# Moving the causal mask of two half batches from TensorE to GpSimd in a fused attention and gated-convolution kernel

## The chip, the cores and the metric

The kernel runs on one core of a Trainium2 chip. A core has a matrix engine (TensorE; PE in the profile, with its weight loads as PEld), a vector engine (VectorE, DVE), an activation engine (ScalarE, ACT), a general engine (GpSimd, POOL), and a queue engine that here only issues transfers (SyncE, SP). Each takes its own instructions in the order written and waits on semaphores for the others. Working tiles lie in SBUF; matrix products land in PSUM, from where ACT or DVE fetch them. POOL reads and writes SBUF only here. The metric is the device time of one execution, in microseconds (us).

## What is computed

Eight batches, eight heads, 576 positions, head width 64. The attention has a decay that is worked out from a forget gate `f`, and a causal mask; its output goes through a feed-forward layer with a three-tap convolution along the sequence and a sigmoid gate.

```python
cum = np.cumsum(np.log(np.clip(f, 0.0001, 1.0)), axis=-1)
scores = scale * q @ k.T + cum[:, None] - cum[None, :]
attn = softmax(np.where(causal, -1e9, scores)) @ v
h = np.maximum(attn @ w_in, 0.0)
conv = w0 * h[s - 1] + w1 * h[s] + w2 * h[s + 1]
out = (h * sigmoid(conv)) @ w_out
```

(Shortened: per head for the attention, per channel for the convolution.)

## The kernel before

Work is cut into 16 half batches of four heads each (`hb`), and each half batch into two pairs of heads, numbered `i = 2*hb` and `2*hb + 1`. The scores are made transposed (keys on partitions, queries along the free axis) in blocks of 128 by 128, and only the blocks on or below the diagonal are made. For each pair there are three batches of scores: `sd` holds the diagonal blocks (two heads, 1024 columns), `so...0` and `so...1` hold the off-diagonal blocks of one head each. For each half batch `st` holds the last 64 positions against themselves for all four heads (256 columns). ACT takes the exponential of each out of PSUM: `ed`, `eo`, `et`. Then `pv` multiplies the result with the values `v`, in two parts (`pv6.0`, `pv6.1`); `n` normalises on DVE; `t` and `tx` transpose the outcome for the feed-forward part. A value tile is first cast to 16 bits by `va`, on the engine that the order names (`va6.0@POOL`).

Only diagonal blocks need the mask. Two ways to apply it are in the code, and `MASK_PE` lists the half batches that use the first:

- on TensorE ahead of the scores: `masked` (line 367) writes a product of an identity and a mask matrix of very negative numbers into PSUM, and the scores are added on top. For a half batch that is four products of 512 columns and one of 256. The exponential then writes the 16-bit tile that `pv` reads.
- on GpSimd behind the exponential: `ed` and `et` write 32-bit tiles instead (`pd_t`, two of them; `p3_t`, two of them), and `md` (line 403) and `mt` (line 382) copy these to the 16-bit tile with zeros in place of what is masked. `pv` then waits for `md` and `mt` instead of `ed` and `et`.

Before the change half batches 0 to 7 use the first way and 8 to 15 the second.

The feed-forward part of each batch is `f` (first product), `r` (relu on ACT), `c` and `d` (the two steps of the convolution on DVE), `a` (tanh on ACT), `g` (gate on DVE), `o` (second product), `e` (copy out of PSUM) and `s` (store).

The order of all this work is a list written out by hand, `ORDER`. Each engine gets its instructions in the order of that list; there is no other scheduler. Buffers are handed out as the list is gone through: `Plan.play` keeps a list of free buffers per kind, a task takes the first free one, and a task that gives one back appends it to the end. PSUM has four buffers (`ps`), `pd` has two, `p3` two. Waits between engines follow from which instruction reads or writes which part of which buffer, transfers included.

Two small buffers live inside larger tiles. `cwrow`, the convolution weights as loaded, lies in `pd_t[0]` and is read at the start. `signs`, two rows of plus and minus ones, lies in `pd_t[1]`:

```python
signs = pd_t[1].rearrange("p s c -> p (s c)").bitcast(BF16)
plus, minus = (signs[0:BH, x * S:(x + 1) * S] for x in range(2))
```

The task `zc` (lines 330 and 331) sends them to a table in DRAM, with transfers issued by GpSimd; from that table, and from a block of zeros sent by the same task, the half batches from 8 on fill rows of their score operands (`fi8` and following, lines 241 and 243, issued by SP):

```python
for j, a, c in ((1, 0, plus), (2, 0, plus), (0, 1, minus), (3, 0, zero[:, 0:S]), (3, 1, zero[:, 0:S])):
    nc.gpsimd.dma_start(image[j, a], c)
nc.gpsimd.dma_start(blank, zero[0:60])
```

Of the kernel before, what the change touches and what calls it, by code (L numbers as in the profile page):

```python
# [17 lines left out]
dca cw ld0 ld0.0.0 tp0.0.0 dcl ld0.1.0 ld0.0.1 tp0.0.1 tp0.1.0 v0.0 ld1 ld0.1.1 ld1.0.1 ld1.0.0 dcs dck q2.1 ki@SP
cl0.0.0@ACT cl0.0.1@ACT v0.4 cl0.1.0@ACT tp0.1.1 q2.0 cwt sd0 ed0 cl0.1.1@DVE tp1.0.0 tp1.0.1 cl1.0.0@ACT cl1.0.1@DVE
tp1.1.0 tp1.1.1 cl1.1.1@ACT sd1 so1.0 eo1.0 cl1.1.0@DVE so0.0 so1.1 rw1 sd2 eo0.0 v0.1 ed1 cl2.1 cl2.0 eo1.1 v0.2 ed2  # L20
v0.3 va1.0@DVE va1.1@DVE rw2 wi1 sd3 so2.0 ed3 so3.1 eo3.1 va0.0@POOL va0.1@POOL so0.1 eo0.1 so3.0 wi0 eo3.0 st0 eo2.0
et0 so2.1 eo2.1 pv0.0 st1 n0.0 et1 q3.0 pv0.1 n0.1 pv1.0 pv1.1 n1.0 n1.1 wic0@ACT wi3 sd4 wic1@POOL ed4 t0 tx0@DVE t1
tx1@DVE sd5 cl3.0 q3.1 cl3.1 so5.1 eo5.1 f0.0 r0.0 f0.1 c0.0 wic3@POOL d0.0 st2 r0.1 ed5 et2 c0.1 d0.1 so4.0 eo4.0 wi2
f0.2 r0.2 v1.0 v1.3 v1.1 wic2@POOL c0.2 d0.2 h0 a0.0 g0.0 v1.4 f0.3 v1.2 f0.4 a0.1 r0.4 f0.5 f0.6 r0.5 va2.0@ACT rw3
sd6 q5.0 so4.1 g0.1 va3.0@DVE q5.1 r0.3 r0.6 c0.5 c0.3 so5.0 c0.4 sd7 d0.4 wo1 ed6 eo5.0 st3 et3 eo4.1 d0.5 cl5.0 a0.2
so7.1 ed7 eo7.1 pv2.0 so7.0 va2.1@DVE pv2.1 cl5.1 n2.0 q4.1 d0.3 va3.1@POOL eo7.0 wo2 rw5 so6.1 eo6.1 woc2@POOL g0.2
so6.0 cl4.1 eo6.0 q4.0 f0.7 r0.7 wo0 woc1@ACT pv3.0 a0.3 a0.5 n2.1 t2 q6.0 n3.0 tx2@ACT c0.7 g0.5 pv3.1 n3.1 a0.4 g0.3
sd11 ed11 so11.1 eo11.1 sd10 so10.1 eo10.1 ed10 cl4.0 rw4 wo3 woc0@ACT t3 tx3@DVE f1.0 r1.0 d0.7 a0.7 c0.6 d0.6 a0.6
f1.1 r1.1 f1.2 g0.4 so11.0 c1.0 v2.0 d1.0 sd8 f1.3 g0.6 r1.2 eo11.0 ed8 cl6.0 g0.7 q6.1 v2.2 r1.3 sd9 ed9 c1.3 d1.3
so8.0 v2.1 f1.4 r1.4 c1.4 d1.4 h1 a1.0 woc3@POOL o0.0 g1.0 eo8.0 cl6.1 st5 et5 a1.4 c1.1 g1.4 d1.1 so10.0 eo10.0 f1.5  # L30
a1.3 g1.3 so9.1 eo9.1 v2.3 va5.0@DVE r1.5 c1.5 d1.5 o0.1 e0.0@ACT f1.6 r1.6 f1.7 r1.7 st4 so9.0 eo9.0 a1.1 va4.0@DVE
pv5.0 q7.0 cl7.0 v2.4 so8.1 va5.1@POOL pv5.1 et4 eo8.1 rw6 q7.1 va4.1@ACT n5.0 sd13 v3.0 v3.4 pv4.0 n5.1 pv4.1 ed13 zc
n4.0 n4.1 a1.5 v3.1 so13.1 sd12 eo13.1 cl7.1 ed12 c1.2 t5 so12.0 eo12.0 t4 tx4@ACT tx5@ACT o0.2 q9.0 c1.7 d1.7 so12.1
eo12.1 a1.7 rw7 o0.3 c1.6 e0.1@ACT f2.0 f2.1 d1.2 d1.6 so13.0 a1.2 g1.5 g1.7 r2.0 f2.2 f2.3 r2.1 q8.1 eo13.0 g1.2 c2.0
st7 a1.6 o0.4 r2.3 g1.1 v3.2 v3.3 q9.1 et7 sd15 d2.0 r2.2 h2 c2.1 a2.0 e0.2@DVE so15.0 so15.1 ed15 g1.6 eo15.0 sd14
ed14 so14.0 eo14.0 f2.4 r2.4 f2.5 va6.0@POOL pv6.0 c2.3 d2.3 q8.0 c2.2 g2.0 so14.1 r2.5 o1.0 eo15.1 va7.0@DVE
va7.1@ACT d2.2 c2.4 st6 eo14.1 pv7.0 a2.2 et6 va6.1@DVE n6.0 pv6.1 d2.1 a2.1 d2.4 n7.0 v4.0 fi9 s0.2 v4.1 c2.5 s0.0
v4.4 fi8 q10.0 s0.1 a2.4 v4.3 n6.1 v4.2 g2.2 o1.1 e1.0@ACT pv7.1 sd19 f2.6 f2.7 q11.0 q10.1 g2.4 ed19 n7.1 r2.6 c2.6
d2.6 r2.7 sd18 ed18 t6 q11.1 t7 o1.2 tx6@DVE tx7@ACT a2.6 a2.3 d2.5 a2.5 g2.1 st9 f3.0 et9 g2.3 f3.1 so19.1 c2.7 d2.7
r3.0 r3.1 a2.7 md19 sd17 ed17 o1.3 f3.2 g2.6 g2.5 c3.0 so19.0 eo19.1 e1.1@DVE r3.2 eo19.0 d3.0 c3.2 o1.4 e1.2@DVE s1.2  # L40
c3.1 d3.1 md18 st8 s1.0 g2.7 fi10 so18.0 fi11 et8 f3.3 va9.0@DVE va9.1@ACT md17 s1.1 v5.0 eo18.0 so17.0 so18.1 h3 d3.2
a3.0 r3.3 eo17.0 a3.1 f3.4 f3.5 f3.6 g3.1 v5.3 v5.1 r3.5 g3.0 o2.0 a3.2 g3.2 c3.3 r3.4 r3.6 sd16 f3.7 eo18.1 mt8 ed16
so16.1 eo16.1 r3.7 d3.3 a3.3 c3.4 d3.4 v5.2 c3.7 d3.7 c3.6 so16.0 eo16.0 o2.1 e2.0@ACT a3.4 pv9.0 a3.7 va8.0@ACT
so17.1 q12.0 n9.0 md16 va8.1@ACT q12.1 eo17.1 o2.2 o2.3 e2.1@ACT st10 et10 c3.5 d3.5 d3.6 mt9 g3.4 pv9.1 n9.1 mt10
pv8.0 pv8.1 a3.5 n8.0 a3.6 n8.1 o2.4 g3.7 q13.0 g3.5 v5.4 e2.2@ACT fi12 s2.2 sd22 ed22 sd20 ed20 md22 t8 tx8@DVE t9
tx9@DVE g3.6 g3.3 q13.1 so20.0 md20 sd23 so22.1 eo20.0 ed23 sd21 md23 va11.0@DVE ed21 f4.0 r4.0 c4.0 d4.0 f4.1 f4.2
r4.1 eo22.1 f4.3 c4.1 r4.2 r4.3 so23.1 eo23.1 h4 so21.1 d4.1 a4.0 g4.0 so23.0 f4.4 r4.4 eo21.1 c4.2 a4.1 s2.1 o3.0
eo23.0 f4.5 v6.0 r4.5 f4.6 d4.2 a4.2 so22.0 md21 g4.1 fi13 eo22.0 c4.4 va11.1@DVE st11 et11 s2.0 mt11 o3.1 c4.5 d4.5
v6.3 so21.0 r4.6 o3.2 v6.1 v6.2 a4.5 so20.1 q14.1 q14.0 eo21.0 e3.0@ACT d4.4 f4.7 eo20.1 c4.6 g4.5 r4.7 sd24 a4.4
pv11.0 ed24 sd25 o3.3 c4.3 d4.3 g4.2 c4.7 d4.7 so25.1 md24 n11.0 pv11.1 ed25 e3.1@ACT va10.0@POOL eo25.1 a4.7 pv10.0  # L50
st12 d4.6 va10.1@POOL pv10.1 et12 sd27 n11.1 n10.0 n10.1 ed27 g4.7 o3.4 t10 e3.2@ACT a4.6 a4.3 t11 sd26 tx10@DVE
tx11@DVE md27 v6.4 ed26 so25.0 so27.1 g4.6 eo27.1 f5.0 f5.1 so26.0 q15.0 r5.0 c5.0 g4.3 d5.0 eo25.0 r5.1 c5.1 f5.2
so24.0 eo26.0 f5.3 f5.4 r5.2 eo24.0 r5.3 g4.4 o4.0 so26.1 so27.0 h5 a5.0 fi14 d5.1 a5.1 r5.4 eo27.0 c5.3 g5.0 d5.3
eo26.1 c5.4 c5.2 s3.2 q15.1 d5.2 so24.1 d5.4 eo24.1 a5.2 g5.1 va12.0@DVE o4.1 f5.5 st13 et13 va12.1@ACT g5.2 f5.6 md25
mt12 md26 r5.5 c5.5 d5.5 f5.7 r5.6 sd28 e4.0@ACT r5.7 c5.7 ed28 pv12.0 n12.0 so28.1 o4.2 pv12.1 a5.5 g5.5 va13.0@ACT
pv13.0 eo28.1 d5.7 a5.3 mt13 sd29 s3.0 md28 o4.3 va13.1@POOL n12.1 ed29 md29 c5.6 n13.0 fi15 pv13.1 a5.4 g5.4 e4.1@ACT
s4.1 n13.1 sd31 ed31 md31 sd30 t12 ed30 d5.6 md30 t13 o4.4 a5.6 tx12@DVE tx13@DVE so31.0 st14 a5.7 g5.6 g5.3 f6.0 et14
mt14 v7.0 eo31.0 r6.0 c6.0 f6.1 r6.1 c6.1 d6.0 f6.2 r6.2 e4.2@ACT so31.1 eo31.1 f6.3 so29.0 so29.1 g5.7 f6.4 r6.3 c6.2
d6.1 d6.2 eo29.0 r6.4 v7.2 c6.4 eo29.1 d6.4 o5.0 so28.0 o5.1 s4.0 h6 a6.1 eo28.0 g6.1 a6.2 st15 f6.5 v7.3 a6.0
e5.0@ACT et15 mt15 s3.1 c6.3 v7.1 va14.0@DVE pv14.0 v7.4 so30.0 s4.2 g6.0 g6.2 r6.5 va15.0@POOL va15.1@ACT eo30.0  # L60
n14.0 so30.1 c6.5 eo30.1 f6.6 r6.6 f6.7 va14.1@POOL pv14.1 d6.5 a6.4 d6.3 n14.1 a6.3 pv15.0 pv15.1 t14 r6.7 c6.6 a6.5
o5.2 n15.0 n15.1 t15 tx14@ACT tx15@ACT c6.7 d6.7 a6.7 d6.6 o5.3 g6.3 g6.7 e5.1@ACT f7.0 f7.1 r7.0 f7.2 o5.4 g6.4 f7.3
g6.5 a6.6 r7.1 c7.0 d7.0 r7.2 e5.2@ACT r7.3 c7.1 d7.1 h7 a7.0 g6.6 c7.2 d7.2 f7.4 f7.5 f7.6 f7.7 g7.0 a7.1 g7.1 r7.6
r7.4 s5.2 o6.0 o6.1 o7.0.0 c7.6 c7.3 r7.5 d7.3 d7.6 a7.2 c7.4 d7.4 a7.3 e6.0@ACT s5.0 g7.3 c7.5 a7.4 g7.2 o6.2 o6.3
o6.4 r7.7 c7.7 d7.5 g7.4 s6.0 o7.2.0 o7.3.0 o7.0.1 o7.0.2 a7.6 o7.2.1 o7.1.0 o7.2.2 e6.1@ACT d7.7 o7.2.3 s5.1 o7.1.1
o7.3.1 o7.1.2 o7.1.3 e6.2@ACT o7.0.3 o7.1.4 o7.2.4 a7.5 g7.6 g7.5 o7.2.5 a7.7 s6.2 s6.1 g7.7 o7.1.5 o7.2.6 o7.2.7
e7.2@ACT s7.2 o7.0.4 o7.0.5 o7.0.6 o7.0.7 o7.1.6 o7.3.2 o7.1.7 e7.0@ACT s7.0 e7.1@DVE o7.3.3 o7.3.4 o7.3.5 o7.3.6
# [39 lines left out]
def kernel(  # L107
# [290 lines left out]
    def diag_exp(i):  # L398
        o = pair(i)[:, :, 0:512] if i // 2 in MASK_PE else pd_t[slot[f"ed{i}", "pd"]]
        nc.scalar.activation(o, ps_of(f"sd{i}").rearrange("p (s c) -> p s c", s=2), AF.Exp, scale=SCALE)  # L400
# [316 lines left out]
```

## Time and profile before

| | us |
|---|---|
| median of three runs | 250.18 (249.65 to 250.89) |
| the profiled execution, its own time | 250.38 |
| its span (first to last instruction) | 248.4 |
| PE busy | 232.6 |
| DVE busy | 215.3 |
| ACT busy | 213.0 |
| POOL busy | 46.2 |

The page of the profile gives busy time by engine, the span in 40 slices, the chain of work that ended last, and the costliest groups of instructions. The timeline lists single instructions or runs of equal ones with start, duration and, in brackets, idle time before them and what ended it. The stretches view gives busy time of each engine between two moments. A matmul's duration reaches past the start of the next, since matmuls are pipelined; the time that one takes up on PE is read from start to start.

### The profile page before, as it was taken

What the parts mean: (1) busy time and instruction counts of PE and PEld (TensorE: products, weight loads), DVE (VectorE), ACT (ScalarE), POOL (GpSimd) and SP (SyncE); (2) the same over time, 40 slices, a digit from 0 to 9 for tenths busy, and PEclk for the clock granted to TensorE, in tenths of its full rate; (3) what the DMA queues carried; (4) which work ended last, traced back from release to release, by engine and by line L of the source; (5) the groups of instructions that cost most, each with busy time, mean ns of one, the idle gap of its engine ahead of it and who ended that gap; (6) DMA issues with size and microseconds to landing.
All of it is one profiled execution on the core that took longest, in us unless ns stands there. A gap on an engine that the chain in (4) does not pass through costs nothing.

```text
span 248.4 us, 6681 instructions
## 1 busy us (share of the span) xinstructions
PE 232.6 (94%) x2768; PEld 150.9 (61%) x2768; DVE 215.3 (87%) x328; ACT 213.0 (86%) x288; POOL 46.2 (19%) x76
## 2 busy tenths in 40 slices
...
GB/s 198 302 193 193 239 211 231 186 271 203 247 212 180 235 198 250 268 219 218 218 261 253 216 174 268 224 235 160 220 229 5 163 305 2 3 3 106 129 145 191
DMA packets 114694, 48.22 MB, mean 194 GB/s; under 512 B 104034, under 2 KB 105250, under 8 KB 114664
## 3 DMA queue, kind: packets, MB, share of 16 engines
...
q0 software_dynamic: 208, 0.51, 0.6%
...
q14 instruction: 9, 0.07, 0.1%
...
## 4 chain that ended last, share of the span: by engine, by line
PE 65%; SPq 9%; DVE 9%; DMA 8%; ACT 3%; issue 3%; ACTq 0%; DVEq 0%
PE ps L504 21%; PE ps L473 19%; PE ps L359 11%; SPq L227 6%; PE ps L436 6%; DMA qk<-in_k_dram 3%; PE ps L508 3%; DVE u L488 3%; DMA qk<-in_q_dram 3%; DVE u L490 2%; DMA u<-in_f_dram 2%; PE ps L458 2%; PE ps L441 2%; DVE hg L497 2%; DVE qk L233 1%
## 5 line engine op out<-in xcount | busy, mean ns | idle before, releaser
L417 ACT ACTIVATE pp<-ps 128x1024 f16<-128x1024 f32 x64 | 65.5, 1044 | 4.9 <-PE ps L359 2.7
L473 PE MATMUL ps<-xt,w_in_f 128*128 128x512 f16 (+1 forms) x512 | 68.2, 286 | 1.0 <-ACT ht L483 0.3
L359 PE MATMUL ps<-qk 128*128 128x128 bf16 (+2 forms) x576 | 63.2, 240 | 1.7 <-DVE xm L450 0.6
L504 PE MATMUL ps<-w_out_f,hg 128*128 128x512 f16 x256 | 59.4, 379 | 0.0
L488 DVE SCALAR_TENSOR_TENSOR u<-ht,cwt 128x576 f32<-128x576 f16 x64 | 52.8, 832 | 2.5 <-ACT ht L483 2.4
L490 DVE SCALAR_TENSOR_TENSOR u<-ht,cwt,u 128x576 f32<-128x576 f16 x64 | 53.7, 852 | 1.4
L473 PEld LDWEIGHTS <-w_in_f 128*128 128x128 f16 x512 | 34.0, 98 | 30.4 <-issue 1.8
L493 ACT ACTIVATE hg<-u,cw 128x576 f16<-128x576 f32 x64 | 48.8, 784 | 2.9 <-DVE u L490 2.9
L497 DVE SCALAR_TENSOR_TENSOR hg<-hg,ht 128x576 f16<-128x576 f16 x64 | 50.3, 806 | 1.1 <-ACT hg L493 0.9
L359 PEld LDWEIGHTS <-qk 128*128 128x128 bf16 x576 | 39.2, 98 | 19.2 <-issue 3.4
L483 ACT ACTIVATE ht<-ps 128x576 f16<-128x576 f32 x64 | 41.2, 668 | 2.9 <-PE ps L473 2.8
L504 PEld LDWEIGHTS <-hg 128*128 128x128 f16 x256 | 24.0, 98 | 25.6 <-issue 0.2
L403 POOL TENSOR_SCALAR_AFFINE_SELECT pp<-pd 128x1024 f16<-128x1024 f32 x16 | 18.5, 1168 | 48.7 <-ACT pd L400 42.9
L450 DVE TENSOR_TENSOR xm<-ps,rc 128x896 f16<-128x896 f32 (+1 forms) x32 | 24.3, 758 | 1.1
L436 PE MATMUL ps<-va,pp 128*128 128x65 f16 x640 | 24.6, 193 | 0.6 <-ACT pp L417 0.4
L436 PEld LDWEIGHTS <-pp 128*128 128x128 f16 x640 | 22.4, 97 | 3.0 <-ACT pp L417 0.7
L400 ACT ACTIVATE pp<-ps 128x1024 f16<-128x1024 f32 x16 | 16.5, 1039 | 4.0 <-PE ps L359 3.0
L514 ACT COPY ob<-ps 128x1024 f32<-128x1024 f32 (+1 forms) x18 | 15.1, 839 | 4.0 <-PE ps L504 3.2
L400 ACT ACTIVATE pd<-ps 128x1024 f32<-128x1024 f32 x16 | 15.9, 1023 | 1.9 <-PE ps L359 1.9
L367 PE MATMUL ps<-mask,ident 128*128 128x512 bf16 (+1 forms) x40 | 14.5, 362 | 0.4 <-ACT xt L464 0.2
L233 DVE TENSOR_SCALAR qk<-qk,lim 128x2304 uint16<-128x2304 uint16 x12 | 10.5, 874 | 3.1 <-DMA qk<-in_q_dram 1.9
L382 POOL TENSOR_SCALAR_AFFINE_SELECT pt<-p 128x256 f16<-128x256 f32 x8 | 4.8, 594 | 38.6 <-ACT p L379 37.0
...
## 6 DMA issues: line engine op xcount, KB each, us to landing
vf<-in_v_dram SPq DMA_DIRECT2D x32, 256.0 KB, 4.9
...
out_dram<-ob SPq DMA_DIRECT2D x4, 256.0 KB, 2.1
...
```

The source lines that it names most:

```text
L359: nc.tensor.matmul(o, tk[:, h * S + k0:h * S + k0 + 128], tq[:, h * S + q0:h * S + q0 + n], start=first, stop=last and not by_matmul(hb, h))
L400: nc.scalar.activation(o, ps_of(f"sd{i}").rearrange("p (s c) -> p s c", s=2), AF.Exp, scale=SCALE)
L417: nc.scalar.activation(pair(i)[:, s, 512:1536], ps_of(f"so{i}.{s}"), AF.Exp, scale=SCALE)
L436: nc.tensor.matmul(ps[:, c:c + D + 1], block(hb, h, m, n), va[:, h, m, 0:D + 1], start=(m == 0), stop=(m == n))
L450: nc.vector.tensor_tensor(xm[:, CUT * D * u:CUT * D * u + nj * k * D].rearrange("p (j x d) -> p j x d", x=k, d=D), got[:, :, :, 0:D], r.un ...
L473: nc.tensor.matmul(ps[:, t0:t1], w_in_f16[:, cc, 128 * ff:128 * (ff + 1)], xt[:, cc, x:x + t1 - t0], start=(cc == 0), stop=(cc == NCC - 1))
L483: nc.scalar.activation(ht_of(b, ff)[:, 1:1 + S], ps_of(f"f{b}.{ff}")[:, 0:S], AF.Relu, scale=0.5)
L488: nc.vector.scalar_tensor_tensor(u, ht[:, 0:S], cwt[:, ff, 0:1], ht[:, 1:1 + S], op0=ALU.mult, op1=ALU.add)
L490: nc.vector.scalar_tensor_tensor(u, ht[:, 2:2 + S], cwt[:, ff, 1:2], u, op0=ALU.mult, op1=ALU.add)
L493: nc.scalar.activation(hg_of(b, ff), u_t[slot[f"c{b}.{ff}", "u"]], AF.Tanh, scale=cw[:, ff, 1:2])
L497: nc.vector.scalar_tensor_tensor(hv, hv, 1.0, ht_of(b, ff)[:, 1:1 + S], op0=ALU.add, op1=ALU.mult)
L504: nc.tensor.matmul(ps[:, 512 * (c % 2):512 * (c % 2 + 1)], hg_of(b, ff)[:, 128 * c:128 * (c + 1)], w_out_f16[:, ff, :], **kw)
```

## The change

Half batches 6 and 7 (pairs 12 to 15) go over from the first way of masking to the second. Ten mask products leave PE; four `md` and two `mt` are added on POOL; the four `ed` and two `et` write 32-bit tiles. Each new task stands in the order right behind the exponential that feeds it; every other task keeps its place relative to the rest. (The list is also written as one line instead of many; only the inserted names differ.)

```diff
-    MASK_PE = (0, 1, 2, 3, 4, 5, 6, 7)
+    MASK_PE = (0,1,2,3,4,5)

 ORDER, where names are inserted:
-va5.1@POOL pv5.1 ... sd13 ... pv4.0 n5.1 pv4.1 ed13 zc n4.0 n4.1 a1.5 v3.1 so13.1
+va5.1@POOL pv5.1 ... sd13 ... pv4.0 n5.1 pv4.1 ed13 md13 zc n4.0 n4.1 a1.5 v3.1 so13.1
-sd12 eo13.1 cl7.1 ed12 c1.2 t5 so12.0 eo12.0 t4 tx4@ACT tx5@ACT o0.2 q9.0
+sd12 eo13.1 cl7.1 ed12 md12 c1.2 t5 so12.0 eo12.0 t4 tx4@ACT tx5@ACT o0.2 q9.0
-st7 a1.6 o0.4 r2.3 g1.1 v3.2 v3.3 q9.1 et7 sd15 d2.0 r2.2 h2 c2.1 a2.0 e0.2@DVE so15.0 so15.1 ed15 g1.6
+st7 a1.6 o0.4 r2.3 g1.1 v3.2 v3.3 q9.1 et7 mt7 sd15 d2.0 r2.2 h2 c2.1 a2.0 e0.2@DVE so15.0 so15.1 ed15 md15 g1.6
-eo15.0 sd14 ed14 so14.0 eo14.0 f2.4 r2.4 f2.5 va6.0@POOL pv6.0
+eo15.0 sd14 ed14 md14 so14.0 eo14.0 f2.4 r2.4 f2.5 va6.0@POOL pv6.0
-st6 eo14.1 pv7.0 a2.2 et6 va6.1@DVE n6.0 pv6.1
+st6 eo14.1 pv7.0 a2.2 et6 mt6 va6.1@DVE n6.0 pv6.1
```

More of the change, by code (lines that the diff above doesn't have):

```diff
@@ L17 @@
 ORDER = """
[L18 to L67, printed above, removed]
```

2 lines of the change are left out of this document (1 added, 1 removed).

## The prediction

> **What bounds the kernel now.** I read the page first, then the stretches of four microseconds around half batches 6 and 7, then the timeline of each engine there.
>
> ```profile
> span 248.4 us, 6681 instructions
> PE 232.6 (94%) x2768; PEld 150.9 (61%) x2768; DVE 215.3 (87%) x328; ACT 213.0 (86%) x288; POOL 46.2 (19%) x76
> PE 65%; SPq 9%; DVE 9%; DMA 8%; ACT 3%; issue 3%; ACTq 0%; DVEq 0%
> ```
>
> The third line is the chain that ended last: TensorE carries most of it. What it loses behind the start it hardly gets back, since it is busy to the end. But the share is an average; in the stretch that the change touches a second engine is just as full:
>
> ```profile
> 84.00:88.00 4.00, 4.00 (x46) 2.84 (x43) 3.93 (x7) 3.43 (x5) 0.00 (x0) 1.00 1.14 208
> 88.00:92.00 4.00, 4.00 (x26) 2.01 (x25) 4.00 (x6) 4.00 (x6) 0.00 (x0) 1.00 0.94 189
> 92.00:96.00 4.00, 4.00 (x46) 2.54 (x45) 3.31 (x6) 4.00 (x7) 0.32 (x1) 1.00 1.13 225
> 96.00:100.00 4.00, 4.00 (x45) 2.68 (x40) 3.69 (x6) 3.94 (x6) 1.21 (x1) 1.00 1.16 250
> 100.00:104.00 4.00, 4.00 (x56) 2.55 (x53) 3.96 (x8) 4.00 (x7) 0.00 (x0) 1.00 1.00 237
> 104.00:108.00 4.00, 4.00 (x76) 2.78 (x74) 3.77 (x6) 2.64 (x5) 0.00 (x0) 1.00 1.16 316
> ```
>
> The columns after the stretch's length are PE, PEld, DVE, ACT and POOL busy, then PE's granted clock and the transfers' share. From 88 to 104 ACT works without a gap, as PE does: a delay of ACT delays everything, and time given to PE alone is worth nothing until ACT has room, from about 106.6 on. POOL is nearly idle.
>
> **The products taken away.** Eight mask products of 512 columns and two of 256 go.
>
> ```profile
> 81.29 0.38 PE L367 MATMUL ps<-mask,ident 128*128 128x512 bf16 x1
> 81.51 0.38 PE L359 MATMUL ps<-qk 128*128 128x128 bf16 x4
> 104.50 0.27 PE L367 MATMUL ps<-mask,ident 128*128 128x256 bf16 x1
> 104.61 0.28 PE L359 MATMUL ps<-qk 128*128 128x64 bf16 x4
> ```
>
> From start to start a large one takes 0.22 us, a small one 0.11: 8 x 0.22 + 2 x 0.11 = 1.98 us. Only the small one of `st6`, at 104.50, lies close to where ACT has room. The rest lies before or inside the stretch in which ACT is full, so I credit 0.1 us; the ends are 0 and 1.98.
>
> **The first new wait: the buffer with the signs.** This is the largest term. The diagonal exponentials now take `pd` buffers. `ed13` takes the first, `pd_t[0]`. `md13` stands ahead of `ed12` in the order and puts `pd_t[0]` back at the end of the list, so `ed12` takes `pd_t[1]`: the tile in which `signs` lies and from which `zc` sends three transfers. `ed12` overwrites it, so it must wait until these have landed. Before, nobody took a `pd` buffer until half batch 9, at 109.68. And `zc` itself comes later, since it is now queued behind `md13` on POOL, which waits for `ed13`. POOL and ACT before:
>
> ```profile
> 78.00 0.67 POOL L266 CAST va<-vf 64x256 f16<-64x256 f32 x1 [9.67 <-DMA vf<-in_v_dram]
> 78.62 2.22 POOL L330 DMA_DIRECT2D image<-pd  x3
> 95.68 1.53 POOL L264 CAST va<-vf 128x1024 f16<-128x1024 f32 x1 [12.99 <-PE ps L508]
> 110.78 1.10 POOL L403 TENSOR_SCALAR_AFFINE_SELECT pp<-pd 128x1024 f16<-128x1024 f32 x1 [13.57 <-ACT pd L400]
> ```
>
> ```profile
> 82.37 1.02 ACT L400 ACTIVATE pp<-ps 128x1024 f16<-128x1024 f32 x1
> 85.55 1.02 ACT L400 ACTIVATE pp<-ps 128x1024 f16<-128x1024 f32 x1
> 87.37 2.15 ACT L464 COPY xt<-ps 128x1152 f16<-128x1152 f16 x2
> 99.22 1.03 ACT L400 ACTIVATE pp<-ps 128x1024 f16<-128x1024 f32 x1
> 100.13 1.04 ACT L417 ACTIVATE pp<-ps 128x1024 f16<-128x1024 f32 x1
> 108.49 1.01 ACT L514 COPY ob<-ps 128x1024 f32<-128x1024 f32 x1 [1.85 <-PE ps L504]
> 109.68 1.02 ACT L400 ACTIVATE pd<-ps 128x1024 f32<-128x1024 f32 x1 [0.18 <-PE ps L359]
> ```
>
> ```profile
> L403 POOL TENSOR_SCALAR_AFFINE_SELECT pp<-pd x16: 1092/1097/1584, 110.8 to 196.5; 128x1024 f16<-128x1024 f32 x16
> L330 POOL DMA_DIRECT2D image<-pd x3: 526/715/998, 78.6 to 79.8; - x3
> DMA to landing us min/median/max: 3.0/3.9/4.9
> ```
>
> The rows of ACT at 82.37 and 85.55 are `ed13` and `ed12`; 99.22 is `ed14`, 100.13 `eo14.0`. `ed13` ends at 83.39. A select follows its exponential by 0.08 (109.68 + 1.02, then 110.78), so `md13` runs from 83.47 to 84.57. Then `zc`: its third transfer starts 1.2 us after its first (78.6 to 79.8), so near 85.7. The last line is the landing time of the five transfers of that line to the table, 3.0 to 4.9 us; I take the median, 3.9, as the third one's own 4.9 was the longest and other traffic differs from one moment to the next. It lands at 89.6, and `ed12` starts near 89.7 instead of 85.55: 4.1 us. The ends are 3.2 (landing 3.0) and 5.1 (landing 4.9), and 5.6 with the longest select.
>
> Behind `ed12` on ACT everything waits: `eo12.0`, the two copies at 87.37, the tanh and relu. TensorE waits too:
>
> ```profile
> 86.69 0.22 PE L459 MATMUL ps<-ident,xm 128*128 128x128 f16 x1
> 86.75 1.89 PE L504 MATMUL ps<-w_out_f,hg 128*128 128x512 f16 x8
> 99.39 2.12 PE L473 MATMUL ps<-xt,w_in_f 128*128 128x512 f16 x16
> 101.35 1.16 PE L436 MATMUL ps<-va,pp 128*128 128x65 f16 x32
> ```
>
> `o0.2`, at 86.75, takes the PSUM buffer that `ed12` empties; before, it started 0.18 after `ed12`'s end at 86.57. Now it starts near 90.9, 4.1 late. ACT has no gap up to 104 in which to catch up.
>
> The price of a GpSimd transfer can also be had elsewhere. The Trainium skill, DMA: Bandwidth & Descriptors, section on the anatomy of one DMA on the gpsimd path, fits about 2.0 us plus the bytes at 436 GB/s; for one of 72 KB that makes an estimated 2.2 us. By that the first wait would be 2.4 and not 4.1 us, and the time about 254.1. The trace's own transfers, 3.0 us at the least, speak against it.
>
> **The second new wait: the cast behind the selects.** In POOL's order `va6.0` (95.68) now stands behind `md15` and `md14`. `pv6.0`, at 101.35 on PE, needs it. In times of before, to which the first delay is added: `ed14` ends at 100.24 + 0.01, `md14` runs from 100.33 to 101.43, and `va6.0` follows. Casts of that form on POOL:
>
> ```profile
> L264 POOL CAST va<-vf x4: 1032/1284/1532, 25.0 to 209.8; 128x1024 f16<-128x1024 f32 x4
> L382 POOL TENSOR_SCALAR_AFFINE_SELECT pt<-p x8: 414/500/923, 122.6 to 209.4; 128x256 f16<-128x256 f32 x8
> ```
>
> With 1.28 it ends at 102.71, and `pv6.0` starts near 102.75: 1.4 late. The ends are 1.1 (cast of 1.03) and 1.7 (1.53). The relu products ahead of `pv6.0`, at 99.39, wait for `eo15.0` on ACT, so the missing mask products don't bring PE there sooner. Behind `pv6.0` stand `so14.1`, `o1.0`, `st6` and so on, and the 1.85 us for which ACT waited at 108.49 was a wait for PE: from here PE sets the pace, and the delay stays.
>
> **The smaller parts.** `mt6` now stands between `et6` and the last products of `pv6.1`, which follow a little later: 0.2 us, ends 0 and 0.5 (the select takes 0.41 to 0.92). `md12`, `md15`, `mt7` have microseconds until `pv6.0` and `pv7.0`; nothing. The exponentials cost the same (1.02 in either form above). The blocks of zeros that `zc` sends land 6 us later; the first reader is at 98.39 on SP:
>
> ```profile
> 82.14 0.55 POOL L331 DMA_DIRECT2D blank<-zero  x1
> 98.39 0.95 SPq L241 DMA_DIRECT2D qk<-blank  x1
> ```
>
> Issued near 88.0 and landed in the 4.9 us that the longest row above took, they are there by 93; without that cover it would cost at most what it is late. A select also slows a product on DVE that runs beside it:
>
> ```profile
> 107.28 0.81 DVE L488 SCALAR_TENSOR_TENSOR u<-ht,cwt 128x576 f32<-128x576 f16 x1
> 111.40 1.09 DVE L488 SCALAR_TENSOR_TENSOR u<-ht,cwt 128x576 f32<-128x576 f16 x1 [0.87 <-ACT ht L483]
> ```
>
> The second lies beside the select of 110.78: 0.28 more. `md15` and `md14` would cost DVE 0.6, and between 92 and 100 it is idle for 1.0 (3.31 and 3.69 of 4.00): covered; 0.6 if not.
>
> **The sum.** 4.1 + 1.4 + 0.2 - 0.1 = 5.6 us. The profiled execution took 250.38 (the span and 1.98 around it), so 256.0; the median is 0.20 lower: 255.8. Its own range: 3.2 + 1.1 - 1.5 (most of the products' gain after all) = 2.8, so 253.0, up to 5.6 + 1.7 + 0.5 = 7.8, so 258.0.
>
> **The rivals.** First, *TensorE comes back slow*. While `ed12` waits, PE has nothing to do: its last work ahead of `o0.2`, moved up by what the products leave free, ends near 86.4, and the next starts near 90.9, a gap of 4.5 us. The only such gap in the trace is at the start, before 6.41:
>
> ```profile
> 7.32 3.06 PE L213 MATMUL ps<-ident_b,hg 128*128 128x128 bf16 x27
> 13.75 2.44 PE L213 MATMUL ps<-ident_b,hg 128*128 128x128 bf16 x36
> ```
>
> The same transposes took (3.06 - 0.22) / 26 = 0.109 us each first and (2.44 - 0.22) / 35 = 0.063 later, though the granted clock is shown as 1.00 in both. Some 36 of these at 0.046 more are 1.7 us. If a gap of 4.5 us does the same, the sum is 7.3 and the time 257.5. Against it: the first gap was longer and nothing had run before. The Trainium skill, TensorE: Matmul & The Clock Gate, Part 1, has the rule: half clock after an idle window of about 3.4 us, until about 3.4 us of work; the window is free-running, so a gap of 4.5 need not hold a whole one. The slow transposes agree, the granted clock doesn't.
>
> Second, *the second wait is absorbed*: if PE comes to `pv6.0` late for another reason, such as a buffer of PSUM that ACT empties later than before, the cast is done by then and only the first wait counts: 255.8 - 1.4 = 254.4. For it: all of PE's products from `o0.2` on depend on an ACT that is full. Against it: `pv6.0` followed without a gap before.
>
> Third, *`ed12` doesn't wait*: the buffers come out the other way, or the transfers have read the signs early. Then only the second wait is left: 250.2 + 1.4 + 0.2 - 0.1 = 251.7. The hand-out of buffers speaks against it.
>
> Fourth, on the other side, *PE's own work decides*: the chain is PE's, each product taken from its queue comes off, 250.2 - 2.0 = 248.2. It needs PE alone to be the bound between 82 and 108, and it decides only if `ed12` waits less than the 2.0 us saved; with a transfer issued near 85.7, after `ed12`'s old start, and 3.0 at the least, it doesn't.
>
> **How the numbers follow.** My forecast 0.62, slow TensorE 0.18, second wait absorbed 0.07, no wait at `ed12` 0.07, faster 0.06. The three runs of before lie 0.5% apart, so 0.5% is about what can be told from no change. Faster 0.06; within 0.5% (251.4 and less) 0.05, from the low edge of the third; slower 0.89. The range 253.0 to 259.0 leaves out the last two (251.7 and 248.2), and the far ends of the others: less than 2 in 10.
>
> **What would show it.** Right: ACT idle for some 4 us ahead of the `ed12` row, ended by a transfer or POOL; PE idle as long ahead of `o0.2`; the `image<-pd` row some 6 us later on POOL; the cast `va6.0` behind two selects, and PE idle for about 1.4 ahead of `pv6.0`. Slow TensorE: `o0.2`'s eight products in some 3.5 us instead of 1.73. Wrong: no idle row on ACT between 83 and 91, or gaps on PE that are made good before 230.

## The result, and the profile after

The change makes the kernel slower: 258.65 us (median of four runs, 256.0 to 259.32) against 250.15, a ratio of 1.0318 with a 95% interval of 1.0282 to 1.0355. The profiled execution took 258.59 us with a span of 256.8, 8.4 more than before. A ratio, here and below, leaves out executions more than 1.5% longer than the fastest of their kernel, which the medians include (with 24 added products on TensorE two of six were left). Below, lines are those of the kernel after, 50 lower than before (L350 is the diagonal exponential into `pd`, L353 the select, L280 the transfers of `zc`, L454 the second product of the feed-forward part, L214 the cast of the values, L438, L440 and L447 the two convolution steps and the gate on VectorE).

Four stretches, the first three of which are shown for before; columns: the stretch, its length, busy PE, PEld, DVE, ACT, POOL, granted clock, transfers' share and rate.

```profile
84.00:88.00 4.00, 2.14 (x32) 1.88 (x31) 3.93 (x7) 1.02 (x1) 3.55 (x7) 1.00 1.11 193
88.00:92.00 4.00, 1.13 (x3) 0.40 (x3) 3.03 (x5) 2.20 (x3) 1.10 (x1) 0.67 1.14 281
92.00:96.00 4.00, 4.00 (x13) 1.57 (x12) 0.00 (x0) 2.44 (x3) 0.00 (x0) 0.50 1.16 189
...
108.00:112.00 4.00, 2.06 (x41) 1.58 (x39) 4.00 (x5) 2.49 (x5) 1.92 (x2) 1.00 0.96 255
```

PE and ACT, full or nearly so before, are idle for more than half of the time from 84 to 92. The granted clock of PE, 1.00 in all these stretches before, falls to 0.67 and 0.50. A second hole on PE follows from 108 to 112. The timelines show what each is. ACT first:

```profile
81.88 1.04 ACT L350 ACTIVATE pd<-ps 128x1024 f32<-128x1024 f32 x1
...
89.80 1.02 ACT L350 ACTIVATE pd<-ps 128x1024 f32<-128x1024 f32 x1 [4.54 <-DMA image<-pd]
```

`ed12`, the row at 89.80, waited 4.54 us, for transfers out of `pd`. It is the only row of ACT that the trace puts down to a transfer of the signs. POOL and the landing times of its transfers:

```profile
83.00 1.10 POOL L353 TENSOR_SCALAR_AFFINE_SELECT pp<-pd 128x1024 f16<-128x1024 f32 x1 [3.94 <-ACT pd L350]
84.05 1.93 POOL L280 DMA_DIRECT2D image<-pd  x3
...
90.90 1.10 POOL L353 TENSOR_SCALAR_AFFINE_SELECT pp<-pd 128x1024 f16<-128x1024 f32 x1 [3.35 <-ACT pd L350]
...
106.85 1.57 POOL L353 TENSOR_SCALAR_AFFINE_SELECT pp<-pd 128x1024 f16<-128x1024 f32 x1 [0.73 <-ACT pd L350]
108.37 1.55 POOL L214 CAST va<-vf 128x1024 f16<-128x1024 f32 x1
```

```profile
L280 POOL DMA_DIRECT2D image<-pd x3: 526/706/715, 84.0 to 85.3; - x3
...
DMA to landing us min/median/max: 3.9/4.4/5.2
```

`md13` (83.00) stands ahead of the three transfers (84.05), the third of which starts at 85.3; `ed12` starts 4.5 us later. The selects `md15` and `md14` and then the cast `va6.0` (108.37) show the second queue; `md14` took 1.57 us and the cast 1.55. PE:

```profile
85.92 0.22 PE L409 MATMUL ps<-ident,xm 128*128 128x128 f16 x1
90.87 3.57 PE L454 MATMUL ps<-w_out_f,hg 128*128 128x512 f16 x8 [4.73 <-ACT pd L350]
94.24 1.06 PE L309 MATMUL ps<-qk 128*128 128x64 bf16 x4
95.09 2.42 PE L454 MATMUL ps<-w_out_f,hg 128*128 128x512 f16 x8
97.35 2.12 PE L423 MATMUL ps<-xt,w_in_f 128*128 128x512 f16 x16
...
109.97 1.15 PE L386 MATMUL ps<-va,pp 128*128 128x65 f16 x32 [1.94 <-POOL va L214]
```

Before, the four products behind `o0.2` and then `f2.0`:

```profile
88.47 0.60 PE L359 MATMUL ps<-qk 128*128 128x64 bf16 x4
...
90.64 2.12 PE L473 MATMUL ps<-xt,w_in_f 128*128 128x512 f16 x16
```

`o0.2`, at 90.87, came 4.73 us after PE had run dry and 4.12 us later than before (86.75). Its eight products took 3.37 us to the next start, instead of 1.72. `f2.0` starts at 97.35, 6.71 late (90.64 before): 2.59 us were lost behind the first wait, while the clock was low. `pv6.0` starts at 109.97, after 1.94 us of waiting for the cast, 8.62 late (101.35 before). The end is 8.4 late: from there on 0.2 us is won back and nothing more is lost. So the profiled 8.4 us are 4.1 (first wait), 2.6 (slow TensorE), 1.9 (second wait), less 0.2 later.

### The profile page after: what moved, and what is told of

It reads as the page before. It is cut to its first block, busy times and chain, and to the rows that moved or that the text cites. A ratio compares the mean times of both kernels' runs of the same rounds, so it can differ in the third digit from the quotient of the medians.

```text
span 256.8 us, 6669 instructions
## 1 busy us (share of the span) xinstructions
PE 233.4 (91%) x2758; PEld 150.4 (59%) x2758; DVE 217.8 (85%) x328; ACT 213.8 (83%) x288; POOL 52.1 (20%) x82
## 4 chain that ended last, share of the span: by engine, by line
PE 60%; ACT 10%; SPq 8%; DMA 7%; issue 5%; DVE 4%; POOL 3%; ACTq 0%; DVEq 0%; POOLq 0%
PE ps L454 22%; PE ps L423 18%; PE ps L309 10%; SPq L177 5%; PE ps L386 5%; DMA qk<-in_k_dram 3%; ACT ht L433 3%; PE ps L458 3%; ACT pp L367 3%; DMA u<-in_f_dram 2%; ACT hg L443 2%; DVE u L438 2%; DMA image<-pd 2%; PE ps L391 2%; PE ps L408 2%
## 5 line engine op out<-in xcount | busy, mean ns | idle before, releaser
L367 ACT ACTIVATE pp<-ps 128x1024 f16<-128x1024 f32 x64 | 65.2, 1041 | 7.2 <-PE ps L309 4.9
L454 PE MATMUL ps<-w_out_f,hg 128*128 128x512 f16 x256 | 61.6, 389 | 4.7 <-ACT pd L350 4.7
L447 DVE SCALAR_TENSOR_TENSOR hg<-hg,ht 128x576 f16<-128x576 f16 x64 | 50.3, 804 | 7.9 <-ACT hg L443 7.7
L440 DVE SCALAR_TENSOR_TENSOR u<-ht,cwt,u 128x576 f32<-128x576 f16 x64 | 54.7, 867 | 1.4
L438 DVE SCALAR_TENSOR_TENSOR u<-ht,cwt 128x576 f32<-128x576 f16 x64 | 52.7, 831 | 2.0 <-ACT ht L433 1.9
L454 PEld LDWEIGHTS <-hg 128*128 128x128 f16 x256 | 24.5, 100 | 31.9 <-issue 7.5
L353 POOL TENSOR_SCALAR_AFFINE_SELECT pp<-pd 128x1024 f16<-128x1024 f32 x20 | 23.4, 1180 | 49.7 <-ACT pd L350 49.7
L350 ACT ACTIVATE pd<-ps 128x1024 f32<-128x1024 f32 x20 | 20.1, 1026 | 6.5 <-DMA image<-pd 4.5
L332 POOL TENSOR_SCALAR_AFFINE_SELECT pt<-p 128x256 f16<-128x256 f32 x10 | 5.7, 570 | 53.4 <-ACT p L329 53.4
L350 ACT ACTIVATE pp<-ps 128x1024 f16<-128x1024 f32 x12 | 12.4, 1044 | 3.4 <-PE ps L309 2.5
L183 DVE TENSOR_SCALAR qk<-qk,lim 128x2304 uint16<-128x2304 uint16 x12 | 11.3, 943 | 3.7 <-DMA qk<-in_q_dram 2.5
L214 DVE CAST va<-vf 128x1024 f16<-128x1024 f32 x9 | 7.9, 876 | 4.2 <-DMA vf<-in_v_dram 4.2
## 6 DMA issues: line engine op xcount, KB each, us to landing
vf<-in_v_dram SPq DMA_DIRECT2D x32, 256.0 KB, 4.6
out_dram<-ob SPq DMA_DIRECT2D x4, 256.0 KB, 2.1
```

The source lines that it names most:

```text
L367: nc.scalar.activation(pair(i)[:, s, 512:1536], ps_of(f"so{i}.{s}"), AF.Exp, scale=SCALE)
L438: nc.vector.scalar_tensor_tensor(u, ht[:, 0:S], cwt[:, ff, 0:1], ht[:, 1:1 + S], op0=ALU.mult, op1=ALU.add)
L440: nc.vector.scalar_tensor_tensor(u, ht[:, 2:2 + S], cwt[:, ff, 1:2], u, op0=ALU.mult, op1=ALU.add)
L447: nc.vector.scalar_tensor_tensor(hv, hv, 1.0, ht_of(b, ff)[:, 1:1 + S], op0=ALU.add, op1=ALU.mult)
L454: nc.tensor.matmul(ps[:, 512 * (c % 2):512 * (c % 2 + 1)], hg_of(b, ff)[:, 128 * c:128 * (c + 1)], w_out_f16[:, ff, :], **kw)
```

## The experiments

Ratios are to the kernel before on the same chip and in the same hours, with 95% intervals; its median was 251.24 us beside the first four kernels, 250.99 beside the one with both waits taken away and the one with 24 added products, and 251.66 beside the one with shorter selects, the kernel after run again and the one with 40 added products.

### The signs in a tile of their own

```diff
-    signs = pd_t[1].rearrange("p s c -> p (s c)").bitcast(BF16)
+    signs = cpool.tile([64, 2 * S], BF16, name="signs")
```

> The signs get a tile of their own, nothing else is changed against the kernel after. Theory (the shared buffer): the 4.5 us wait of ACT ahead of ed12 goes, and with it the gap and the slow products on TensorE; the wait of pv6.0 for its cast on GpSimd, 1.9 us, stays. 250.2 + 1.9 = 252.1 us, between 251.2 and 252.9; granted clock 1.00 throughout. Rival (GpSimd's selects are dear in themselves, by their time between exponential and product and by slowing VectorE): most of the 8.5 us stays, 256 us or more.

Measured: 255.11 us, ratio 1.0174 (1.0116 to 1.0232). The wait ahead of `ed12` is gone, and `o0.2` follows at once, but the loss is some 2 us more than I expected (3.9 us by the medians, not 1.9). PE:

```profile
86.80 1.89 PE L454 MATMUL ps<-w_out_f,hg 128*128 128x512 f16 x8
...
104.09 1.46 PE L386 MATMUL ps<-va,pp 128*128 128x65 f16 x32 [1.93 <-POOL va L214]
105.36 1.05 PE L309 MATMUL ps<-qk 128*128 128x64 bf16 x4
106.20 2.85 PE L454 MATMUL ps<-w_out_f,hg 128*128 128x512 f16 x8
```

`pv6.0` waits 1.93 us for its cast, as foreseen. But then the clock falls to half, and the next products run slow: `o1.0`'s eight take 2.68 us from start to start (106.20, next at 108.88) instead of 1.72, the four of `so14.1` 0.84 instead of 0.44. With `pv6.0` itself (1.27 instead of 0.99) that is 1.6 us. So a gap of 1.9 us was enough here, while the same gap in the kernel after left the clock at 1.00.

Where the gap lies decides. Within each trace the moments at which the clock changes lie a multiple of 3.41 us apart: it is at half from 104.72 to 108.13 here, and from 89.33 to 96.16 in the kernel after. Two stretches of 3.41 us of this run, then the one of the kernel after in which most of its second gap lies (counted on from 96.16):

```profile
101.31:104.72 3.41, 1.48 (x29) 1.03 (x28) 3.41 (x4) 2.53 (x5) 2.73 (x2) 1.00 1.03 231
104.72:108.13 3.41, 3.41 (x26) 1.90 (x23) 3.38 (x6) 2.05 (x4) 0.00 (x0) 0.50 1.09 237
```

```profile
106.40:109.81 3.41, 1.64 (x14) 0.83 (x13) 3.41 (x4) 2.53 (x5) 2.96 (x2) 1.00 1.04 309
```

Here the whole gap lies in one such stretch, PE was busy for only 1.48 us of it, and the next is at half. In the kernel after the gap reaches over the end of the stretch at 109.81, 1.64 us of work were left in it, and the next stayed at 1.00. All eleven traces of this case agree: a stretch at full clock with 1.48 us or less of busy PE is followed by half clock, one with 1.59 us or more by full clock. The mean clock, which every execution has, suggests that the fall is no rarity: 0.991 in all four here, 1.000 in all four of the next kernel.

### The signs sent first

```diff
-... pv4.1 ed13 md13 zc n4.0 ...
+... pv4.1 ed13 zc md13 n4.0 ...
```

> The signs stay in the pd buffer; only zc goes ahead of md13 in the order, so that its transfers are issued near 78.6 us as before. Theory: the transfers land near 84.7, no later than ed12 can start, so the wait ahead of ed12 is under 0.5 us and the time is that of the kernel with signs of their own, 251.2 to 253.0. If instead the sharing of the buffer costs something whatever the moment of the transfer, ACT still waits for a microsecond or more there, and the time is 254 or more.

Measured: 253.75 us, ratio 1.0104 (1.0058 to 1.0149). PE:

```profile
88.87 1.89 PE L454 MATMUL ps<-w_out_f,hg 128*128 128x512 f16 x8 [1.10 <-ACT pd L350]
...
105.35 1.15 PE L386 MATMUL ps<-va,pp 128*128 128x65 f16 x32 [1.75 <-POOL va L214]
106.34 0.60 PE L309 MATMUL ps<-qk 128*128 128x64 bf16 x4
106.77 1.89 PE L454 MATMUL ps<-w_out_f,hg 128*128 128x512 f16 x8
```

The shared buffer costs 1.1 us ahead of `o0.2` now. ACT waited 0.91 us for `ed12`, which lies between my two expectations: the transfers were issued from 82.0 and not from 78.6, since the cast ahead of them on GpSimd came at 81.25 instead of 78.00. (The trace puts this wait down to PE's transposes, which ended at the same moment; nothing in the order makes `ed12` wait for these.) Measured from the moment at which ACT was ready for `ed12`, the third transfer starts 3.6 us earlier than in the kernel after, and the wait is 3.6 us shorter: it was for the moment of the transfer, and the sharing by itself costs nothing that shows. The wait of `pv6.0` is there, 1.75 us, and this time the clock stayed: 0.43 and 1.73 to the next starts. Moving one name in the order takes away two thirds of the loss.

### One half batch alone

```diff
-    MASK_PE = (0,1,2,3,4,5)
+    MASK_PE = (0,1,2,3,4,5,6)       # and md13 md12 mt6 out of the order
```

> Half batch 7 alone is masked on GpSimd, half batch 6 stays on TensorE. Theory: ed14 takes the buffer with the signs long after they have landed, so no first wait and no slow products; the cast va6.0 still stands behind md15 and md14, so pv6.0 waits for 1.4 to 1.9 us: 251.2 to 252.6. Rival (each half batch on GpSimd costs the same): half of 8.5, 254.4.

```diff
-    MASK_PE = (0,1,2,3,4,5)
+    MASK_PE = (0,1,2,3,4,5,7)       # and md15 md14 mt7 out of the order
```

> Half batch 6 alone is masked on GpSimd, half batch 7 stays on TensorE. Theory: the whole first wait, 4.1 us, and the slow products behind it, 2.6 us, are there; the cast va6.0 has no select ahead of it on GpSimd but those of half batch 6, long done: 250.2 + 6.7 = 256.9, between 255.5 and 257.7. Rival (each half batch on GpSimd costs the same): 254.4.

Measured: half batch 7 alone 253.34 us, ratio 1.010 (1.0066 to 1.0134); half batch 6 alone 260.08, ratio 1.0355 (1.0296 to 1.0414). The two don't cost the same: the rival falls. Half batch 7 costs its wait: PE waits for the cast for 1.9 us in that run. (The mean clock was 0.991 or 0.992 in four of its ten executions and 0.997 or 0.998 in the others, so the clock fell behind this wait in some of them, as far as a mean can tell.) Half batch 6 costs more alone than I expected, as much as both together. ACT, then POOL:

```profile
94.01 1.02 ACT L350 ACTIVATE pd<-ps 128x1024 f32<-128x1024 f32 x1 [7.33 <-DMA image<-pd]
```

```profile
85.57 2.22 POOL L280 DMA_DIRECT2D image<-pd  x3
```

The wait was 7.33 us here and not 4.54: the third transfer, issued at 86.8, let `ed12` start only at 94.01, 7.2 us later. The landing time of these transfers is not a constant of the kernel.

### Both waits taken away

```diff
+    signs = cpool.tile([64, 2 * S], BF16, name="signs")     # as above
-... v3.3 q9.1 et7 mt7 sd15 ... f2.5 va6.0@POOL pv6.0 ...
+... v3.3 q9.1 va6.0@POOL et7 mt7 sd15 ... f2.5 pv6.0 ...
```

> Signs in a tile of their own, and the cast va6.0 moved ahead of mt7, md15 and md14 in the order, so that GpSimd does it as soon as its values are loaded. Theory: both new waits are gone. What is left is 2.0 us less on TensorE, most of it hidden by a full ACT, against slower products on VectorE beside the selects: 249.5 to 250.6. Rival (the selects cost by themselves): 251.5 or more.

Measured: 253.93 us, ratio 1.0118 (1.0076 to 1.016). My theory missed. PE waits for GpSimd nowhere, and the clock stays at 1.00 in every stretch from 86 to 116, yet 1.2% of loss is left. VectorE before, then in this kernel, with POOL beside it:

```profile
99.32 0.81 DVE L488 SCALAR_TENSOR_TENSOR u<-ht,cwt 128x576 f32<-128x576 f16 x1
...
100.72 0.69 DVE L264 CAST va<-vf 128x1024 f16<-128x1024 f32 x1
101.32 0.81 DVE L490 SCALAR_TENSOR_TENSOR u<-ht,cwt,u 128x576 f32<-128x576 f16 x1
```

```profile
100.82 1.59 DVE L438 SCALAR_TENSOR_TENSOR u<-ht,cwt 128x576 f32<-128x576 f16 x1
...
103.21 1.58 DVE L214 CAST va<-vf 128x1024 f16<-128x1024 f32 x1
104.72 1.64 DVE L440 SCALAR_TENSOR_TENSOR u<-ht,cwt,u 128x576 f32<-128x576 f16 x1
```

```profile
100.55 1.25 POOL L214 CAST va<-vf 128x1024 f16<-128x1024 f32 x1 [9.89 <-issue]
...
102.64 3.10 POOL L353 TENSOR_SCALAR_AFFINE_SELECT pp<-pd 128x1024 f16<-128x1024 f32 x2
```

The convolution steps, 0.81 us each before, take 1.59 and 1.64 beside the cast and the selects on POOL, and the value cast 1.58 instead of 0.69; the selects themselves 1.55 each instead of 1.10. In all VectorE was busy 4.2 us longer than before (215.3):

```profile
PE 232.5 (92%) x2758; PEld 151.2 (60%) x2758; DVE 219.5 (87%) x328; ACT 213.5 (85%) x288; POOL 53.4 (21%) x82
```

That this reaches TensorE shows a little later: PE waits twice, 1.1 us in all, until VectorE has taken an outcome of `pv` out of PSUM into the tile `xm`.

```profile
111.35 0.61 PE L309 MATMUL ps<-qk 128*128 128x128 bf16 x8 [0.47 <-DVE xm L400]
112.62 2.12 PE L423 MATMUL ps<-xt,w_in_f 128*128 128x512 f16 x16 [0.67 <-DVE xm L400]
```

### Shorter selects

```diff
     def diag_mask(i):
+        if i < 16:
+            nc.gpsimd.affine_select(pair(i)[:, 0, 0:128], pd_t[slot[f"ed{i}", "pd"]][:, 0, 0:128], ...)
+            return
```

> Signs of their own and the cast first, as before, but the four selects md12 to md15 are cut to 128 of their 1024 columns, so that half batches 6 and 7 get wrong scores in most diagonal blocks; everything else, waits included, is kept. Theory (what is left of the loss is VectorE slowed beside the selects): VectorE is busy for 216.5 us or less instead of 219.5, and the time is within 0.5% of before, a ratio of 0.996 to 1.005 instead of 1.012. Rival (something else in these half batches costs it): the ratio stays at 1.010 or more.

Measured: 252.13 us, ratio 1.0024 (0.9984 to 1.0065), where full selects gave 1.0118. (Lines behind the added ones are 4 higher in this kernel, and in the two with added products.)

```profile
PE 231.2 (92%) x2758; PEld 150.1 (60%) x2758; DVE 216.8 (86%) x328; ACT 213.1 (85%) x288; POOL 50.5 (20%) x82
```

```profile
99.72 0.81 DVE L442 SCALAR_TENSOR_TENSOR u<-ht,cwt 128x576 f32<-128x576 f16 x1
...
101.12 1.53 DVE L214 CAST va<-vf 128x1024 f16<-128x1024 f32 x1
```

VectorE's busy time falls to 216.8, 0.3 more than I had set (the cast at 101.12 still lies beside a cast on POOL). By the medians the loss is gone within what can be measured, so what was left with both waits removed goes with the length of the selects. That they act through VectorE is shown in part: TensorE waited for a select in neither kernel, and its two waits for `xm` are gone in this one. But its trace, of an execution of 252.70 us, still has a wait ahead of the same products, `sd19`:

```profile
111.13 0.61 PE L309 MATMUL ps<-qk 128*128 128x128 bf16 x8 [1.32 <-DMA qk<-blank]
```

This transfer fills rows of half batch 9. SP issued it at 104.32, against 98.39 before, and as late with full selects (104.30), where PE waited for `xm` at this place. So how much of the loss goes by way of VectorE alone stays open.

### TensorE kept busy in the gap

```diff
+    def keep_busy():
+        for x in range(24):
+            nc.tensor.matmul(ps_of("t4")[:, 640:1024], w_in_f16[:, 0, 0:128], w_in_f16[:, 1, 0:384],
+                             start=True, stop=True, skip_group_check=True)
-... so12.0 eo12.0 t4 tx4@ACT ...
+... so12.0 eo12.0 t4 kb tx4@ACT ...
```

> The kernel after, with 24 products of 384 columns added on TensorE behind t4, into the unused part of the PSUM buffer of t4; no result uses them. They fill some 3.8 us of the gap of 4.7 us in which TensorE waits for ed12. Theory (the gap lowers the clock): the granted clock stays at 1.00, o0.2 takes 1.9 us instead of 3.57, and the time falls by 2 to 2.6 us, to 256.0 to 256.7. Rival (TensorE is slow there for another reason, or ACT would have been as late anyway): 258 to 259.3.

Measured: 262.61 us (257.82 to 264.38), ratio 1.034 (1.0267 to 1.0413). This decided nothing: the transfers landed late again, so that the added products ended long before `ed12`, and a gap of 3.13 us was left, behind which the clock fell as before:

```profile
87.32 4.06 PE L290 MATMUL ps<-w_in_f 128*128 128x384 f16 x24
94.51 3.00 PE L458 MATMUL ps<-w_out_f,hg 128*128 128x512 f16 x8 [3.13 <-ACT pd L354]
```

So I ran 40 of them, beside the kernel after itself on the same chip.

> The changed kernel itself, to stand beside the next two on the same chip. Theory: the wait of ACT ahead of ed12 is as long as the transfers of the signs take to land, 4.4 us in its first trace but 7 in two relatives; so ACT waits 4.5 to 7.5 us, the granted clock falls to 0.50 behind it, and the time is 258 to 262 us.

> As with 24 added products, but 40, some 6.4 us, so that TensorE is idle for less than 1.5 us ahead of o0.2 however late the signs land; no result uses the added products. Theory (the clock falls because of the gap): the granted clock stays at 1.00 from 86 to 100 us, and o0.2 takes 1.9 us instead of 3.57. The time is then 2 to 2.8 us under the kernel after where the signs land late; where they land at 90 us, the added products hold o0.2 up by some 3 us and the time is the same. Rival (the products are slow there for another reason): o0.2 takes 3 us or more all the same.

Measured: the kernel after 259.59 us, ratio 1.0311 (1.0233 to 1.0389); with 40 added products 260.15, ratio 1.0349 (1.0284 to 1.0413). PE in the kernel after, then with the products:

```profile
87.65 0.22 PE L409 MATMUL ps<-ident,xm 128*128 128x128 f16 x1
95.14 3.50 PE L454 MATMUL ps<-w_out_f,hg 128*128 128x512 f16 x8 [7.27 <-ACT pd L350]
98.48 0.60 PE L309 MATMUL ps<-qk 128*128 128x64 bf16 x4
...
100.64 2.12 PE L423 MATMUL ps<-xt,w_in_f 128*128 128x512 f16 x16
```

```profile
86.56 0.22 PE L413 MATMUL ps<-ident,xm 128*128 128x128 f16 x1
86.61 6.66 PE L290 MATMUL ps<-w_in_f 128*128 128x384 f16 x40
94.79 1.89 PE L458 MATMUL ps<-w_out_f,hg 128*128 128x512 f16 x8 [1.51 <-ACT pd L354]
96.51 0.60 PE L313 MATMUL ps<-qk 128*128 128x64 bf16 x4
...
98.68 2.12 PE L427 MATMUL ps<-xt,w_in_f 128*128 128x512 f16 x16
```

Behind a gap of 7.27 us `o0.2` takes 3.34 us from start to start; behind one of 1.51 us 1.72, and the granted clock stays at 1.00 in all stretches from 86 to 110. So the gap is what lowers the clock, and from `o0.2` to `f2.0` it costs 5.50 - 3.89 = 1.6 us there. The medians don't show this gain: in the profiled runs `o0.2` came 0.7 us later with the added products (8.23 us behind the last transpose, against 7.49), as ACT waited 7.83 us for the transfers instead of 7.08. Whether the added products make the transfers slower, or this is chance, stays open.

No kernel here beats the one before.

## Why the prediction was right, and where it wasn't

The direction, the two waits and their places were right; the likeliest case, 255.8 us, was 2.9 too low. Its own range ended at 258.0. The time lies only in the stated range, which went on to 259.0, and most of what carried it there is a term that the likeliest case had put at nothing: TensorE coming back slow.

- *The first new wait* was sized at 4.1 us, and `o0.2` came 4.12 late. Both halves of the reason hold: a tile for the signs takes the wait away, and so does, but for 1.1 us, sending them ahead of `md13`. The ends, 3.2 to 5.6, were too narrow: I took them from five transfers of one execution, and in other runs `ed12` started up to 7.8 us after the third transfer. That the size fits so well is in part luck: run again, the same kernel waited 7.08 us on ACT instead of 4.54.
- *The second new wait* was sized at 1.4 with an end of 1.7, and measured 1.94. I took `md14` at its median, 1.10, and the cast at its median, 1.28; they took 1.57 and 1.55, with VectorE working beside them.
- *TensorE comes back slow* is the term that failed. I had it as a rival at 0.18 and 1.7 us, since the only such gap in the trace was at the start; it took place and cost 2.6. The Trainium skill, TensorE: Matmul & The Clock Gate, Part 1, speaks of half clock after an idle window of about 3.4 us: the gap of 4.73 us agrees, and so does the granted clock of 0.50. The gap of 1.93 us in the kernel with signs of its own doesn't: the clock fell behind it too, once TensorE was already at work again, with 1.48 us of work in the 3.41 us ahead of the fall. One argument of mine against this rival was a misreading. The clock shown as 1.00 for the slow transposes at the start is no record: the first one in the trace begins at 12.16, and transposes start 0.107 us apart ahead of it and 0.056 behind it, as at half and at full clock.
- *The products taken away* were credited with 0.1 us, and the kernel after shows 0.2 at most (`f2.0` starts 6.71 late, `f2.4` 6.52, at 105.91 instead of 99.39). Between the waits they bring PE earlier to the next wait, no further.
- *A select also slows a product on DVE* was sized at 0.28 us, from one row in which the two overlapped in part, and called covered. With full overlap it is about 0.8 (1.59 against 0.81), and as soon as the two waits are gone, little covers it: 2.9 us are left by the medians, of which shorter selects leave 0.5. In the kernel after VectorE was busy 2.5 us longer as well (217.8), but the three parts above leave nothing of the 8.4 us for it.
- *The smaller parts*, the zeros sent later, the 32-bit exponentials and `mt6` (sized at 0.2), cost nothing that a row of the kernel after shows: `mt6` ends at 114.40, and the products that read its tile follow at 114.73 without idle time on PE.

The fourth rival, PE's own work decides, is excluded by all runs: none is faster than before. The second, the second wait absorbed, didn't happen: PE waited 1.94 us there. The third, only the second wait left, is what half batch 7 alone measures: 1.010, or 252.7 on the 250.15 of before, against the 251.7 that I gave.
